# Attention and MLP on one core: where the tiles begin in a partition

## The chip, the cores and the metric

The kernel runs on one core of one Trainium2 chip. The metric is the device time of one execution in microseconds (us); lower is better.

## What is computed

Eight batches, eight heads, 576 positions, head size 64. Attention is causal by blocks of 64 positions, and its output goes through a layer norm and a two-layer MLP with a residual:

```python
scores = q @ k.T / sqrt(64);  scores = where(block_i >= block_j, scores, -1e9)
attn = exp(scores - max);     attn = attn / (sum(attn) + 1e-9)
x = (attn @ v).transpose(0, 2, 1, 3).reshape(8, 576, 512)
xn = (x - mean(x)) / sqrt(var(x) + 1e-6) * g_ln
out = x + relu(xn @ w_ch1) @ w_ch2          # 512 -> 2048 -> 512
```

All is float32.

## The kernel before

The work is cut into tasks; a planner written in Python (`Plan.run`) simulates the five engines and writes out one fixed order for each. There are two large parts.

**Attention**, 32 pairs of heads. For each pair TensorE makes the scores (`s`, line 388) in plain float32, VectorE adds the mask and takes the maximum (line 403), ScalarE takes the exponential (line 406), TensorE transposes the result (`tr`, line 415) and multiplies it with `v` (`o`, lines 421 and 425). The first block of each head goes a way of its own (lines 527 to 552). In the same time the MLP's weights are loaded and decoded, each into a high and a low part (`w1h`, `w1l`, `w2h`, `w2l`).

**MLP**, 9 groups of 512 rows, 16 steps `j` in each. Its operands have the type `fp32r`. The normalised rows lie in a high and a low part of a tile `xq` (groups 0, 2, 4, 6, 8) or `xp` (groups 1, 3, 5, 7). A step has 12 matmuls into `hp` (lines 675 to 677), a ReLU on ScalarE that writes the high part of `hhl` (line 683), a subtraction on VectorE that writes its low part (line 685), and 12 matmuls into `y` (lines 692 to 694), which TensorE runs after the `hp` of a later step:

```python
nc.tensor.matmul(hp.t, w1h[:, c, jf], xh.t[:, c], start=(c == 0), stop=False)
...
nc.tensor.matmul(ys[s].t, hh.t[:, sl], w2h, start=(j == 0), stop=False)
```

The second operand is the stationary one, 128 columns, which is loaded ahead of its matmul (the rows call this load `PEld`); the third is the moving one, which streams through. In each of these matmuls the moving operand is 512 columns of 4 bytes that lie in a row: 2048 bytes in each partition, and its start is the start of its tile plus a multiple of 2048. So `hp` streams `xq` or `xp`, and `y` streams `w2h` or `w2l`.

SBUF is handed out from the pools in the order in which they are opened, within a pool in the order in which tags are first used, each tile right behind the one ahead of it. The constants end at byte 1152 of a partition; `sums_all` (1024 bytes), `ident` (512), `never` (4352) and `g_sb` (2048) follow, so that the first weight tile begins at 9088 = 4 x 2048 + 896, and all tiles of a multiple of 2048 bytes behind it keep that 896, until a tile of another size comes. The tiles begin here (bytes past a multiple of 2048, and in brackets past a multiple of 256):

| tiles | before | changed |
|---|---|---|
| weights, `pt0`, `st_w2h`, `st_w2l` | 896 (128) | 0 (0) |
| `pu`, `hhl`, `v0` | 896 (128) | 0 (0) |
| `pab`, `xp`, `pt1`, `xre`, `ot`, `xrf`, `xn`, `xt` and their like | 1088 (64) | 0 (0) |
| `xnt`, `xq` | 1344 (64) | 0 (0) |
| `raw`, `qk0`, `wr` (two buffers) | 896, 1408 (128) | 0, 512 (0) |
| `v` (two buffers) | 1920, 384 (128) | 1024, 1536 (0) |
| `ident`, `never`, `g_sb` | 128, 640, 896 (128) | the same |

Of the kernel before, what the change touches and what calls it, by code (L numbers as in the profile page):

```python
# [9 lines left out]
F32 = mybir.dt.float32  # L10
F32R = mybir.dt.float32r
I32 = mybir.dt.int32
# [6 lines left out]
P = 128  # L19
# [35 lines left out]
class Plan:  # L55
# [5 lines left out]
    def add(self, eng, cost=None, fn=None, r=(), w=(), prio=0.0, size=0, alloc=(), mode=128):  # L61
        k = Task(eng if isinstance(eng, dict) else {eng: (cost, fn)}, prio, size)
        k.mode = mode
        before = {}
        for x in r:
            before.update(dict.fromkeys(x.writers))
        for x in w:
            before.update(dict.fromkeys(x.readers))
        for x in r:
            x.readers.append(k)  # L70
        for x in w:
            x.writers.append(k)
        for x in before:
            x.next.append(k)
        k.left = len(before)
        k.uses = list(dict.fromkeys(x.root for x in (*r, *w, *alloc)))
        for x in k.uses:
            x.users += 1
        k.allocs = [x for x in dict.fromkeys(x.root for x in (*w, *alloc)) if x.make]
        self.tasks.append(k)  # L80
        return k
# [101 lines left out]
def attn_mlp_kernel(ctx: ExitStack, tc: tile.TileContext, qk, qk0, v, v0, w1, w2, g, out):  # L183
# [9 lines left out]
    NPAIR, _, _, S = qk.shape  # L193
# [8 lines left out]
    const = ctx.enter_context(tc.tile_pool(name="const", bufs=1))  # L202
    sb = ctx.enter_context(tc.tile_pool(name="sb", bufs=1))
    dram = ctx.enter_context(tc.tile_pool(name="dram", bufs=2, space=bass.MemoryType.DRAM))
    psum = ctx.enter_context(tc.tile_pool(name="psum", bufs=1, space=PSUM))
    plan = Plan()
    add = plan.add

# [14 lines left out]
    def kind(name, shape, dtype, bufs, space=None, tag=None):  # L223

        tag = tag or name
        plan.free.setdefault(tag, bufs)

        def make():
            return (space or sb).tile(shape, dtype, name=name, tag=tag, bufs=bufs)

        def new():
            x = Buf((tag,), make)
            if tag not in ("tr", "x"):
                x.after, last[tag] = last.get(tag), x
            return x
        return new
# [3 lines left out]
    steps = {}  # L240
    new_tr, new_s1, new_hp, new_o = (kind(n, [P, 512], F32, 4, psum, "tr") for n in ("tr", "s1", "hp", "o"))

    new_raw, new_qk0 = kind("raw", [P, 2, S], F32, 2), kind("qk0", [P, 8, 2, 64], F32, 2, None, "raw")
    new_v = kind("v", [P, 5, P], F32, 2)
    new_pab, new_xp = kind("pab", [P, 2048], F32, 2), kind("xp", [P, NC, TW], F32R, 2, None, "pab")
    new_pu, new_hhl = kind("pu", [P, 1024], F32, 2), kind("hhl", [P, 2, 512], F32R, 2, None, "pu")
    new_pt0 = [kind("pt0", [P, 2, 4, 2, P], F32, 1, const, t) for t in ("w1h3", "w1l3")]
# [6 lines left out]
    new_xw = kind("xw", [512, P], F32, 8, dram)  # L254
    new_v0 = kind("v0", [P, 512], F32, 1)
    new_xq = kind("xq", [P, NC, TW], F32R, 2)
    new_nm = kind("nm", [P, 8], F32, 6)
    sums_all = const.tile([P, B, 4, 4, 2], F32, name="sums_all")
    new_st = kind("st", [P, 8], F32, 2)
    new_norm = kind("norm", [P, 16], F32, 3)  # L260
    xd = [kind("xd", [4 * P, 512], F32, B, dram)() for _ in range(B)]
    xd0 = [kind("xd0", [P, DM], F32, B // 2, dram)() for _ in range(B // 2)]

# [6 lines left out]
    gb = Buf()  # L270
    gsrc = bass.AP(tensor=g.tensor, offset=g.offset, ap=[[0, P], [1, DM]])
    add("SP", .45, lambda: nc.sync.dma_start(out=g_sb, in_=gsrc), w=[gb], prio=150, size=P * 2048)
    if WARM:
        warm = new_tr()

        def rouse():
            for _ in range(WARM):
                nc.tensor.transpose(warm.t[:, 0:P], ident, ident)
        add("PE", .2 * WARM + .5, rouse, w=[warm], prio=0)
# [12 lines left out]

    stages = ["w2h3", "w2l3"]
    new_stage = {n: kind("st_" + n, [P, 2048], I32, 1, const, n) for n in stages}
    new_word = kind("wr", [P, 1024], I32, 2, None, "raw")
    staged, staged_last = [0], []

    def decode(j, second, prio, k=0, parts=1):
# [413 lines left out]
def _run_one(arrays):  # L712
    import numpy as np
    import concourse.bacc as bacc
    from concourse.bass_utils import run_bass_kernel_spmd

    nc = bacc.Bacc("TRN2", target_bir_lowering=False, num_devices=1, dynamic_dma_scratch_size=1024)
    args = {n: nc.dram_tensor(n, a.shape, mybir.dt.from_np(a.dtype), kind="ExternalInput").ap()
            for n, a in arrays.items()}
    for n in ("w1", "w2"):  # L720
        args[n] = args[n].bitcast(I32)
    args["out"] = nc.dram_tensor("out_t", (36, P, 512), F32, kind="ExternalOutput").ap()
    with tile.TileContext(nc) as tc:
        attn_mlp_kernel(tc, *args.values())
    r = run_bass_kernel_spmd(nc, [arrays], core_ids=[0])
    return np.asarray(r.results[0]["out_t"])
# [35 lines left out]
```

## Time and profile before

| | us |
|---|---|
| median of 3 runs | 1117.52 (1116.17 to 1118.71) |
| the profiled execution | 1117.89 |
| its span, first to last instruction | 1116.1 |
| outside the span (difference) | 1.8 |

TensorE is busy in 99% of the span, VectorE in 47%, ScalarE in 32%, GpSimd in 12%; the mean share of the DMA engines is 33%. [...]

### The profile page before, as it was taken

To read this page: it belongs to the slowest core of one execution; us is meant where nothing else is said; L and a number is where in the kernel's file an instruction comes from. 1 tells how busy PE (TensorE), PEld (TensorE's weight loads), DVE (VectorE), ACT (ScalarE), POOL (GpSimd) and SP (SyncE) were. 2 spreads that over 40 slices of the span, in tenths; PEclk is the share of its full clock that TensorE was granted. 3 is DMA by queue.
4 is the path that set the end of the run, shared out by engine and by line. 5 is a ranking of instruction groups with operands and counts; after the bars stand their busy time and mean duration, and the time that the engine had idled before them with its cause. 6 is when DMAs were issued, how large, how long until landed. Compare 5 with 4: busy or idle time off the path is not lost.

```text
span 1116.1 us, 16345 instructions
## 1 busy us (share of the span) xinstructions
PE 1102.7 (99%) x6288; PEld 874.0 (78%) x6288; DVE 526.8 (47%) x1244; ACT 356.4 (32%) x880; POOL 130.0 (12%) x192
## 2 busy tenths in 40 slices
PE   9999999999999999999999999999999999999998
PEld 6767777777777888888888888888888888888886
DVE  6899988888866144135126126116215314412111
ACT  7989898997632111111111101111111111111110
POOL 1223423330035001001001001000000100100000
PEclk9999999999999999999999999999999999999999
DMA  6687765664263043034015006005105203301000
GB/s 206 208 200 238 225 221 184 207 194 147 83 149 98 1 87 64 1 72 80 1 49 102 1 13 127 13 0 118 34 1 104 48 1 83 69 1 39 1 1 38
DMA packets 205086, 97.80 MB, mean 88 GB/s; under 512 B 155728, under 2 KB 184400, under 8 KB 205008
## 3 DMA queue, kind: packets, MB, share of 16 engines
q1 hardware_dynamic: 205008, 96.76, 32.6%
q8 instruction: 49, 0.80, 0.3%
q14 instruction: 29, 0.24, 0.1%
HBM read 68.42 MB, written 28.31 MB: 87 GB/s over the span
## 4 chain that ended last, share of the span: by engine, by line
PE 82%; DVE 7%; ACT 6%; issue 2%; DMA 1%; POOL 1%; SPq 1%; DVEq 0%; POOLq 0%; ACTq 0%
PE hp L676 12%; PE hp L677 12%; PE hp L675 12%; PE y L693 11%; PE y L692 11%; PE y L694 11%; PE s L388 4%; PE tr L415 3%; PE o L425 3%; ACT pab L406 2%; ACT pt L217 2%; ACT pu L406 2%; PE o L421 1%; DVE pab L403 1%; DVE pu L403 1%
## 5 line engine op out<-in xcount | busy, mean ns | idle before, releaser
L685 DVE SCALAR_TENSOR_TENSOR hhl<-hp,hhl 128x512 fp32r<-128x512 f32 x144 | 99.6, 691 | 488.4 <-ACT hhl L683 488.3
L683 ACT ACTIVATE hhl<-hp 128x512 fp32r<-128x512 f32 x144 | 86.1, 598 | 695.2 <-PE hp L677 690.9
L694 PE MATMUL y<-w2h,hhl 128*128 128x512 f32 x576 | 224.3, 389 | 2.1 <-DVE hhl L685 2.1
L693 PE MATMUL y<-w2l,hhl 128*128 128x512 f32 x576 | 225.7, 392 | 0.0
L692 PE MATMUL y<-w2h,hhl 128*128 128x512 f32 x576 | 224.7, 390 | 0.0
L694 PEld LDWEIGHTS y<-w2h,hhl 128*128 128x128 f32 x576 | 108.2, 188 | 25.9 <-DVE hhl L685 2.8
L692 PEld LDWEIGHTS y<-w2h,hhl 128*128 128x128 f32 x576 | 108.0, 188 | 25.3
L693 PEld LDWEIGHTS y<-w2l,hhl 128*128 128x128 f32 x576 | 108.0, 188 | 23.7
L675 PE MATMUL hp<-xq,w1h 128*128 128x512 f32 x320 | 126.5, 395 | 0.0
L676 PE MATMUL hp<-xq,w1h 128*128 128x512 f32 x320 | 126.1, 394 | 0.0
L677 PE MATMUL hp<-xq,w1l 128*128 128x512 f32 x320 | 126.1, 394 | 0.0
L675 PE MATMUL hp<-xp,w1h 128*128 128x512 f32 x256 | 100.9, 394 | 0.0
L676 PE MATMUL hp<-xp,w1h 128*128 128x512 f32 x256 | 100.9, 394 | 0.0
L677 PE MATMUL hp<-xp,w1l 128*128 128x512 f32 x256 | 100.9, 394 | 0.0
L388 PE MATMUL s<-raw 64*128 64x320 f32 (+4 forms) x640 | 95.4, 439 | 0.7 <-DVE nm L403 0.6
L406 ACT ACTIVATE pab<-pab,nm 128x576 f32<-128x576 f32 (+1 forms) x128 | 91.5, 729 | 4.1 <-DVE nm L403 4.0
L388 PEld LDWEIGHTS s<-raw 64*128 64x128 f32 x640 | 58.3, 189 | 38.6 <-issue 32.4
L403 DVE CUSTOM_DVE_ANT_0 pab<-s,never 128x576 f32<-128x576 f32 (+1 forms) x128 | 82.6, 684 | 2.1 <-PE s L388 2.1
L425 PE MATMUL o<-pt,v 128*64 128x256 f32 (+1 forms) x768 | 80.4, 344 | 0.0
L425 PEld LDWEIGHTS o<-pt,v 128*64 128x64 f32 x768 | 56.9, 137 | 26.0
L658 POOL TENSOR_TENSOR norm<-norm 128x4 f32<-128x4 f32 x27 | 10.7, 398 | 570.2 <-DVE norm L652 568.8
L217 ACT COPY pt<-tr 128x512 f32<-128x512 f32 x139 | 72.0, 587 | 2.6 <-PE tr L415 2.5
(95 smaller groups left out, 1275.3 us busy)
## 6 DMA issues: line engine op xcount, KB each, us to landing
raw<-qk SPq DMA_DIRECT2D x32, 576.0 KB, 5.0
v<-v SPq DMA_DIRECT2D x32, 320.0 KB, 3.2
xw<-xnt SPq DMA_DIRECT2D x144, 64.0 KB, 2.0
xt<-xw SPq DMA_DIRECT2D x36, 256.0 KB, 2.8
xd<-ot SPq DMA_DIRECT2D x32, 256.0 KB, 3.9
st_w2h<-w SPq DMA_DIRECT2D x14, 512.0 KB, 5.3
st_w2l<-w SPq DMA_DIRECT2D x14, 512.0 KB, 4.7
xrf<-xd SPq DMA_DIRECT2D x80, 64.0 KB, 2.5
```

The costliest lines, as they stand in the source:

```text
L217: e.copy(out=out, in_=in_)
L388: nc.tensor.matmul(x, raw.t[HALF[h], 0, col], raw.t[HALF[h], 1, at:at + x.shape[1]], start=True, stop=True)
L403: add("DVE", dve(n) + .01, lambda: nc.vector.tensor_tensor_reduce(out=p.t[:, part(i, h)], in0=s.t[:, cols], in1=hide, scale=-0.125, scalar ...
L406: add("ACT", act(n, True) + .14, lambda: nc.scalar.activation(out=p.t[:, part(i, h)], in_=p.t[:, part(i, h)], func=AF.Exp, bias=nm.t[:, at ...
L425: nc.tensor.matmul(o.t[HALF[h], at + lo:at + 256], v_sb.t[:, ck, HALF[h]], rhs(h), start=False, stop=(n == len(steps) - 1), skip_group_che ...
L675: nc.tensor.matmul(hp.t, w1h[:, c, jf], xh.t[:, c], start=(c == 0), stop=False)
L676: nc.tensor.matmul(hp.t, w1h[:, c, jf], xl.t[:, c], start=False, stop=False)
L677: nc.tensor.matmul(hp.t, w1l[:, c, jf], xh.t[:, c], start=False, stop=(c == NC - 1))
L685: add("DVE", dve(TW), lambda hp=hp, hh=hh, hl=hl: nc.vector.scalar_tensor_tensor(out=hl.t, in0=hp.t, scalar=0.0, in1=hh.t, op0=ALU.max, op ...
L692: nc.tensor.matmul(ys[s].t, hh.t[:, sl], w2h, start=(j == 0), stop=False)
L693: nc.tensor.matmul(ys[s].t, hh.t[:, sl], w2l, start=False, stop=False)
L694: nc.tensor.matmul(ys[s].t, hl.t[:, sl], w2h, start=False, stop=(j == NJ - 1))
```

## The change

No instruction is added, removed or moved: with line numbers left aside, the two programs have the same instructions in the same order on every engine, with the same waits. What differs is the addresses in SBUF. A pool `odd` is opened last, and the tiles whose size is no multiple of 2048 bytes go there (`raw`, `qk0`, `wr`, `nm`, `st`, `norm`), or, for `v`, into the first pool, where two buffers of 2560 bytes and 128 bytes of padding (`even`) bring the weights to 14336 = 7 x 2048. All else behind that keeps a multiple of 2048; the table above has the starts. PSUM is as before.

```diff
     psum = ctx.enter_context(tc.tile_pool(name="psum", bufs=1, space=PSUM))
+    odd = ctx.enter_context(tc.tile_pool(name="odd", bufs=1))
...
-    new_raw, new_qk0 = kind("raw", [P, 2, S], F32, 2), kind("qk0", [P, 8, 2, 64], F32, 2, None, "raw")
-    new_v = kind("v", [P, 5, P], F32, 2)
+    new_raw, new_qk0 = kind("raw", [P, 2, S], F32, 2, odd), kind("qk0", [P, 8, 2, 64], F32, 2, odd, "raw")
+    new_v = kind("v", [P, 5, P], F32, 2, const)
...
-    new_nm = kind("nm", [P, 8], F32, 6)
+    new_nm = kind("nm", [P, 8], F32, 6, odd)
     sums_all = const.tile([P, B, 4, 4, 2], F32, name="sums_all")
-    new_st = kind("st", [P, 8], F32, 2)
-    new_norm = kind("norm", [P, 16], F32, 3)
+    new_st = kind("st", [P, 8], F32, 2, odd)
+    new_norm = kind("norm", [P, 16], F32, 3, odd)
...
+    const.tile([P, 32], F32, name="even")
...
-    new_word = kind("wr", [P, 1024], I32, 2, None, "raw")
+    new_word = kind("wr", [P, 1024], I32, 2, odd, "raw")
```

## Rows read from the trace of the kernel before

**Rows 1.** Stages: length, busy time (instructions) by engine, granted clock, DMA share, GB/s

```profile
0.00:300.00 300.00, 293.32 (x2727) 218.10 (x2728) 256.31 (x775) 254.26 (x698) 79.81 (x73) 1.00 0.64 197
300.00:339.02 39.02, 36.91 (x218) 29.04 (x216) 28.63 (x55) 13.97 (x30) 14.30 (x20) 1.00 0.54 122
339.02:1110.12 771.10, 771.09 (x3341) 626.11 (x3342) 239.13 (x412) 88.16 (x153) 35.88 (x100) 1.00 0.20 43
1110.12:1116.10 5.98, 1.35 (x6) 0.77 (x5) 2.73 (x4) 0.00 (x0) 0.00 (x0) 1.00 0.46 175
```

**Rows 2.** The chain that ended last, from 339.1 to 1110.1 us: shares by line

```profile
by line: PE hp L676 16.8%; PE hp L677 16.8%; PE hp L675 16.8%; PE y L693 16.6%; PE y L692 16.5%; PE y L694 16.5%
```

**Rows 3.** Matmuls of hp (first row), then of y, in the last stage

```profile
339.02:1112.00 772.98, 410.26 (x1668) 1.00 0.20 43
...
339.02:1112.00 772.98, 404.52 (x1678) 1.00 0.20 43
```

**Rows 4.** TensorE in order of time, a step with xq: start, duration, line

```profile
499.31 0.39 PE L675 MATMUL hp<-xq,w1h 128*128 128x512 f32 x1
...
502.11 0.39 PE L692 MATMUL y<-w2h,hhl 128*128 128x512 f32 x1
```

**Rows 5.** The same, a step with xp, and ScalarE's ReLU of that step

```profile
587.92 0.39 PE L675 MATMUL hp<-xp,w1h 128*128 128x512 f32 x1
...
590.49 0.39 PE L677 MATMUL hp<-xp,w1l 128*128 128x512 f32 x1
590.73 0.39 PE L692 MATMUL y<-w2h,hhl 128*128 128x512 f32 x1
590.95 0.40 PE L693 MATMUL y<-w2l,hhl 128*128 128x512 f32 x1
...
592.11 0.39 PE L692 MATMUL y<-w2h,hhl 128*128 128x512 f32 x1
...
593.24 0.39 PE L694 MATMUL y<-w2h,hhl 128*128 128x512 f32 x1
593.47 0.39 PE L675 MATMUL hp<-xp,w1h 128*128 128x512 f32 x1
...
590.92 0.60 ACT L683 ACTIVATE hhl<-hp 128x512 fp32r<-128x512 f32 x1 [4.94 <-PE hp L677]
```

**Rows 6.** The chain in a head pair: start, length, instructions

```profile
31.41 2.77 PE tr L415 x24
...
34.87 1.51 PE o L425 x16
...
36.82 0.65 PE o L425 x8
```

**Rows 7.** Weight loads: busy us, mean ns of one, idle before

```profile
L675 PEld LDWEIGHTS hp<-xp,w1h 128*128 128x128 f32 x256 | 47.9, 187 | 11.4
...
L415 PEld LDWEIGHTS tr<-ident,pab 128*128 128x128 f32 x512 | 55.3, 141 | 3.9 <-ACT pt L217 1.3 <-issue 0.2
```

**Rows 8.** VectorE's writes of hhl and xq: ns min/median/max

```profile
L685 DVE SCALAR_TENSOR_TENSOR hhl<-hp,hhl x144: 651/692/693, 316.3 to 1106.7; 128x512 fp32r<-128x512 f32 x144
...
L643 DVE TENSOR_TENSOR xq<-xt,xq x20: 650/691/693, 85.9 to 969.3; 128x512 fp32r<-128x512 f32 x20
```

**Rows 9.** The chain ahead of the last stage

```profile
334.97 1.40 DVE w1h L219
...
336.97 1.32 issue
338.29 0.69 DVE hhl L685
...
339.03 0.50 PE y L694
```

**Rows 10.** TensorE's waits from 339.1 to 1110.1 us, all of them

```profile
PE y L694 <- DVE hhl L685: 2.1, 1, 2.1
```

## The prediction

> **What bounds the kernel now.** I read the stages first, then the chain that ended last, then single matmuls. The stages [rows 1] show attention to about 300 us, a mixed stretch to 339.02, an MLP stage of 771.10 us, and a tail of 5.98. In the MLP stage TensorE is busy throughout, VectorE for 239.13 us of it and ScalarE for 88.16; the granted clock is 1.00, which is 2.4 GHz. The chain in that stage [rows 2] is nothing but the six matmul lines, three of `hp` and three of `y`, and the only wait of TensorE on another engine listed there is the one that ends as the stage begins [rows 10]. So 69% of the span is the number of these matmuls times the distance between their starts. The reader should look at that distance, since the change moves no instruction and can act only through addresses.
>
> Twelve `hp` matmuls take 502.11 - 499.31 = 2.80 us when they stream `xq` and 590.73 - 587.92 = 2.81 us with `xp` [rows 4, 5]: 233.3 ns each, at 2.4 GHz 560 clocks for 512 columns. The last six `y` of the step take 593.47 - 592.11 = 1.36 us [rows 5], 226.7 ns each, 544 clocks. What differs between the two kinds? Not the load of weights for the next matmul: from the last `hp` to the first `y`, while `hhl` is loaded, it is 590.73 - 590.49 = 0.24 us, and from the last `y` to the next `hp`, while `w1h` is loaded, 593.47 - 593.24 = 0.23; the rounding allows 233 and 227, so the distance goes with what the matmul itself streams. Both kinds stream 2048 contiguous bytes of the same type. But `xq` and `xp` begin 64 bytes past a multiple of 256, and `w2h` and `w2l` 128 past. I count clocks above 512: 48 for the offset 64, 32 for the offset 128.
>
> One reading fits both with no free constant: the stream is fetched to the end of the 256-byte block in which its last byte lies, at one 4-byte column a clock. From 64 it runs over 2048 + 192 bytes, 560 columns; from 128 over 2048 + 128, 544. It is inferred from two offsets only, so I keep others below.
>
> Plain float32 in attention is a check. There a column takes two clocks, and a fetch with a little surplus would stay hidden. L425 has 16 instructions on `pt0` (offset 128) in 1.51 us and 8 on `pt1` (offset 64) in 0.65 [rows 6]. They run as two heads side by side: 8 streams, six of 256 and two of 128 columns, and 4 streams, two of each. At two clocks a column that is 1493 and 640 ns; 17 and 10 ns are left, 2 to 3 ns for a stream at either offset. So float32 matmuls show no cost of the offset, and a floor of about 2.5 ns that nothing here removes.
>
> **The change part by part.** All parts are addresses, and they come in three kinds.
>
> *What the MLP streams.* `xq`, `xp` and the four `w2` parts all go to offset 0. By the reading above nothing is left above 512 columns: 213.3 ns, plus the 2.5 ns floor seen in attention, 215.8. The stage has 1668 `hp` and 1678 `y` [rows 3]. The saving is 1668 x (233.33 - 215.83) = 29.2 us and 1678 x (226.67 - 215.83) = 18.2 us, in all 47.4. Bounds: without the floor 213.3 ns, 33.4 + 22.4 = 55.7 us; if a sixteen-column unit stays over (560 and 544 are both multiples of 16), 528 columns or 220.0 ns, 22.2 + 11.2 = 33.4 us. I take 215.8, since the floor is in rows.
>
> [...]
>
> *What TensorE loads, and what other engines touch.* A weight load of `hp` is recorded with 187 ns [rows 7], under 215.8, and the record is no floor on the distance: 24 transposes with loads of 141 ns each run in 2.77 us, 115 ns each [rows 6, 7]. VectorE takes 692 ns to write `hhl` (offset 128) and 691 to write `xq` (offset 64) [rows 8], so its time does not hang on the offset: nothing. The first `y` of a step are a little slow: from 590.73 to 592.11 six take 1.38 us, not 1.36, while ScalarE writes `hhl` from 590.92 to 591.52 [rows 5]. That is 0.02 us in each of 139 steps, some 2.8 us in all, which could go or stay; I leave it.
>
> *Attention and its loads.* `raw`, `v`, `pab` and the staging tiles begin at multiples of 256 now. TensorE is idle for 300 - 293.32 = 6.7 us of that stage [rows 1], so no faster transfer or evacuation can give more than that. No row prices a loss. The matmuls there show no cost of the offset, so I take 0.
>
> What hides the rest: of the 9 x 16 x 24 = 3456 MLP matmuls 3346 come after 339.02 and 110 before, and there the chain runs through VectorE's cast of 1.40 us, 1.32 us of issue, and the subtraction at 338.29 [rows 9]. Shorter matmuls ahead of it only wait longer, so I count nothing for them. After it VectorE is needed for 239 of what would be 724 us; no wait follows from that load.
>
> Sum, against the profiled execution: 1117.89 - 47.4 = 1070.5 us. That execution is 0.4 us above the median of the runs, so about 1070 for a median.
>
> **The rivals.**
>
> *Only the odd 64 bytes cost.* Fixed 32 clocks for every `fp32r` matmul, from whatever source (the load of the next weights, say, which ends 187 ns after it starts, leaving some 40 ns to the next `y`), and 16 more when a stream begins off a multiple of 128 bytes. This fits as well, with two constants. For it: `y` is already at a multiple of 128. Against it: float32 shows no such fixed part with loads of the same size. Then `hp` falls to 226.7 and `y` stays: 1668 x 6.67 = 11.1 us, 1106.8 us.
>
> *One unit is left over.* The 220.0 ns worked out above: 1084.5 us.
>
> *Addresses don't matter, the change does nothing.* `hp` and `y` also go to different PSUM tiles, and that could make the 6.7 ns. For it: the tiles of both kinds are contiguous, and every engine row I compared takes the same at both offsets. Against it: clocks above 512 that fit the offsets to the clock. 1117.9 us.
> [...]
>
> *Slower: the surplus grows towards offset 0.* Two points, 48 clocks at 64 and 32 at 128, lie on a line that gives 64 at 0, as if a stream that begins on a block still fetched one block more. Then all matmuls take 576 clocks, 240.0 ns: 1668 x 6.67 + 1678 x 13.33 = 33.5 us more, 1151.4 us. It decides for slower as soon as the surplus at 0 is above 40 clocks, the mean of now. Against it: no byte of that block is needed. For it: no tile begins at 0 now, so no row shows that case.
>
> **How the numbers follow.** Chances: 215.8 ns at both kinds 0.56 (its own range 1058 to 1076: the floor gone, the slow `y` gone, or some transfer in attention better or worse); one unit left 0.07; `hp` alone 0.18; nothing 0.11; slower 0.08. A measurement of this kernel can tell about 0.2% from no change, 2.2 us. Faster is 0.56 + 0.07 + 0.18 = 0.81, the same 0.11, slower 0.08. The range for 8 in 10 holds the first three, from 1058 to 1109.
>
> **What would show it.** In the changed trace twelve `hp` from the first L675 row to the first L692 row of a step (two lines further down in the changed file): 2.59 us if right, 2.72 for `hp` alone, 2.80 for nothing, 2.88 for slower; the twelve `y` after it 2.59 to 2.61 against 2.74 now. Attention must end where it ended, near 300 us, and the first unbroken `hp` stream begin near 339. The chain of the MLP stage must still be six matmul lines; if VectorE's subtraction or a transfer shows in it, the shorter distance has uncovered a wait. The prediction is wrong if `y` does not move: then the offset of 128 cost nothing, and the 32 clocks have another source.

## The result, and the profile after

| | before | changed |
|---|---|---|
| median of 4 runs each, us | 1118.12 (1116.17 to 1118.90) | 1103.95 (1103.25 to 1105.42) |
| the profiled execution, us | 1117.89 | 1104.63 |
| its span, us | 1116.1 | 1102.8 |

The ratio of the times is 0.9878, with a 95% interval of 0.9860 to 0.9896: about 1.2% faster. The forecast was 1070, so the direction was right and the gain 14 us where 48 were expected.

The stages of the changed kernel, to set beside [rows 1] (length, busy us and instructions of PE, PEld, DVE, ACT and POOL, granted clock, DMA share, GB/s):

```profile
0.00:300.00 300.00, 292.96 (x2722) 217.03 (x2723) 256.17 (x775) 253.56 (x696) 79.39 (x73) 1.00 0.63 196
300.00:339.57 39.57, 37.23 (x222) 29.56 (x220) 29.16 (x55) 14.50 (x32) 14.35 (x20) 1.00 0.53 123
339.57:1096.90 757.33, 757.33 (x3341) 627.32 (x3342) 239.49 (x412) 88.16 (x153) 35.28 (x100) 1.00 0.20 44
1096.90:1102.80 5.90, 1.39 (x7) 0.81 (x5) 2.73 (x4) 0.00 (x0) 0.00 (x0) 0.97 0.46 178
```

The whole difference lies in the third row. With 3341 matmuls in both traces the MLP stage takes 757.33 us in place of 771.10, 13.8 less. It begins 0.55 us later (339.57, before 339.02), and the tail is 0.08 shorter: -13.8 + 0.55 - 0.08 = -13.3, which is 1102.8 - 1116.1.

Matmuls recorded with 0.39 us start about 0.23 us apart, so their records overlap; what one takes is counted here from its start to the next one's. TensorE of the changed kernel in order of time, two `y` groups with an `hp` group (on `xp`) between them. All files that are two lines longer than the one before have `hp` at L677 to L679 and `y` at L694 to L696:

```profile
581.33 0.39 PE L694 MATMUL y<-w2h,hhl 128*128 128x512 f32 x1
...
582.69 0.39 PE L694 MATMUL y<-w2h,hhl 128*128 128x512 f32 x1
...
584.05 0.39 PE L677 MATMUL hp<-xp,w1h 128*128 128x512 f32 x1
...
586.77 0.39 PE L694 MATMUL y<-w2h,hhl 128*128 128x512 f32 x1
```

Twelve `hp` take 586.77 - 584.05 = 2.72 us, where [rows 5] had 2.81: 226.7 ns each, 544 clocks. (A clock is 1/2.4 = 0.417 ns here, as in the prediction, at a granted clock of 1.00. Float32 streams take two of these for a further column: the two L425 pieces of [rows 6] differ by four streams of 256 columns, (1.51 - 0.65) us / 4 = 215 ns, and `full` in experiment 1 has 20.60 us / 48 = 429 ns for 512, so 0.84 ns a column.) Twelve `y` take 584.05 - 581.33 = 2.72 us, where they took 2.74. Of these the first six take 1.36 us (before 1.38) and the last six 1.36, as before. So `hp` fell to what `y` had, `y` stayed, and its slow beginning is gone.

The chain of that stage, by line, then TensorE's waits in it (us in total, times, longest), and the chain ahead of it (start, length, what):

```profile
by line: PE y L696 16.7%; PE y L695 16.7%; PE hp L678 16.7%; PE hp L679 16.7%; PE hp L677 16.7%; PE y L694 16.7%
```

```profile
PE y L696 <- DVE hhl L687: 2.3, 1, 2.3
```

```profile
335.51 1.40 DVE w1h L220
...
337.52 1.31 issue
338.84 0.69 DVE hhl L687
...
339.57 0.50 PE y L696
```

These answer to [rows 2, 10, 9]. Still six matmul lines, now with equal shares, and no wait that was not there before.

By terms: 1668 `hp` x 6.67 ns = 11.1 us. The `y` of the stage come in 131 unbroken runs (a few runs hold two steps), and the first six of each run took 0.02 us more before: 2.6 us. Together 13.7, against 13.8 in the stage.

### The profile page after: what moved, and what is told of

Read it like the earlier page. It is cut to its first block, busy times and chain, and to the rows that moved or that the text cites. A ratio compares the mean times of both kernels' runs of the same rounds, so it can differ in the third digit from the quotient of the medians.

```text
span 1102.8 us, 16345 instructions
## 1 busy us (share of the span) xinstructions
PE 1088.9 (99%) x6288; PEld 874.7 (79%) x6288; DVE 527.6 (48%) x1244; ACT 356.2 (32%) x880; POOL 129.0 (12%) x192
## 4 chain that ended last, share of the span: by engine, by line
PE 81%; DVE 8%; ACT 5%; DMA 2%; issue 2%; POOL 1%; SPq 0%; DVEq 0%; ACTq 0%; POOLq 0%
PE y L696 11%; PE hp L678 11%; PE hp L679 11%; PE hp L677 11%; PE y L695 11%; PE y L694 11%; PE s L390 3%; PE o L427 3%; PE tr L417 3%; ACT pab L408 2%; ACT pt L218 2%; ACT pu L408 2%; PE o L423 2%; DVE pab L405 1%; DVE pu L405 1%
## 5 line engine op out<-in xcount | busy, mean ns | idle before, releaser
L696 PE MATMUL y<-w2h,hhl 128*128 128x512 f32 x576 | 224.3, 389 | 2.3 <-DVE hhl L687 2.3
L694 PE MATMUL y<-w2h,hhl 128*128 128x512 f32 x576 | 224.1, 389 | 0.0
L696 PEld LDWEIGHTS y<-w2h,hhl 128*128 128x128 f32 x576 | 108.2, 188 | 25.5 <-DVE hhl L687 3.1
L694 PEld LDWEIGHTS y<-w2h,hhl 128*128 128x128 f32 x576 | 108.2, 188 | 22.5
L677 PE MATMUL hp<-xq,w1h 128*128 128x512 f32 x320 | 124.9, 390 | 0.0
L678 PE MATMUL hp<-xq,w1h 128*128 128x512 f32 x320 | 124.5, 389 | 0.0
L679 PE MATMUL hp<-xq,w1l 128*128 128x512 f32 x320 | 124.5, 389 | 0.0
L677 PE MATMUL hp<-xp,w1h 128*128 128x512 f32 x256 | 99.6, 389 | 0.0
L678 PE MATMUL hp<-xp,w1h 128*128 128x512 f32 x256 | 99.6, 389 | 0.0
L679 PE MATMUL hp<-xp,w1l 128*128 128x512 f32 x256 | 99.6, 389 | 0.0
```

The lines of the kernel that those rows point to most:

```text
L678: nc.tensor.matmul(hp.t, w1h[:, c, jf], xl.t[:, c], start=False, stop=False)
L679: nc.tensor.matmul(hp.t, w1l[:, c, jf], xh.t[:, c], start=False, stop=(c == NC - 1))
L696: nc.tensor.matmul(ys[s].t, hl.t[:, sl], w2h, start=False, stop=(j == NJ - 1))
```

## Experiments

The result leaves 544 clocks for both kinds at offset 0, so "fetched to the end of the 256-byte block" is gone: it asked for 512. Two theories were set against each other; both give 560 clocks for the old `hp` and 544 for all other settled fp32r matmuls of the two traces.

- *Edge*: only the moving operand's own start counts. A stream that begins off a multiple of 128 bytes costs 16 clocks; 32 are paid always.
- *Relation*: while a matmul streams, TensorE loads the stationary operand of the next one: in the trace of the kernel before, the load for the `y` that starts at 590.73 us [rows 5] is recorded from 590.49 on, the start of the `hp` ahead of it (the line below), and loads are busy for 626.11 us of the 771.10 in which the matmuls follow each other without a break [rows 1]. What counts is the distance from the stationary operand's start to the moving one's, modulo 256 bytes. In the kernel before it is 64 - 128, that is 192, for `hp` (`xq` or `xp` against `w1`) and 128 - 128 = 0 for `y` (`w2` against `hhl`).

```profile
590.49 0.19 PEld L692 LDWEIGHTS y<-w2h,hhl 128*128 128x128 f32 x1
```

**1. Matmuls by themselves, at many starts.** A small kernel: 24 equal matmuls, back to back, for each of 37 settings.

```python
COUNT = 24
...
x, s = a[:, o // 4:o // 4 + n], b[:, p // 4:p // 4 + m]
for _ in range(COUNT):
    nc.tensor.matmul(ps[0:m, 0:n], s, x, start=True, stop=True)
```

> This kernel computes nothing of the reference: it runs 24 equal matmuls in a row for each of 37 settings (start of the moving operand, start of the stationary one, columns, type) and writes a dummy output. Edge theory (a stream that begins off a multiple of 128 bytes costs 16 clocks more, and an fp32r matmul of 512 columns has 32 clocks of another source): 226.7 ns between starts with the moving operand at 0, 128, 256 and 1024 bytes, 233.3 at 64, 192 and 320, whatever the start of the stationary one. Relation theory (what counts is where the stream begins relative to the load that runs beside it): 226.7 only where both begin alike, so moving 64 with stationary 64 gives 226.7, and stationary 64 with moving 0 gives 233.3. If the 32 clocks come from the load of the next weights, 64 or 32 stationary columns bring 512 columns to about 216 ns; if they come from the stream, the number of columns sets them, and 480 columns show another surplus. Plain float32 at 0 and at 64 bytes: the same, as in attention.

Its chain (start, length, setting, instructions), with 24 matmuls in each row but the float32 ones, which are recorded as two instructions each:

```profile
14.14 5.44 PE mova L53 x24
...
30.74 5.49 PE movd L53 x24
...
41.84 5.60 PE movf L53 x24
...
53.06 5.60 PE movh L53 x24
58.66 5.46 PE movi L53 x24
...
86.17 5.60 PE stad L53 x24
...
108.30 5.48 PE botha L53 x24
113.78 5.48 PE bothb L53 x24
119.26 5.60 PE bothc L53 x24
...
133.09 2.93 PE lenb L53 x24
136.01 4.17 PE lenc L53 x24
140.18 4.96 PE lend L53 x24
145.13 5.20 PE lene L53 x24
150.33 5.37 PE lenf L53 x24
155.70 2.83 PE odda L53 x24
...
173.21 5.51 PE wida L53 x24
...
184.28 5.20 PE half L53 x24
189.48 20.60 PE full L53 x48
210.08 20.61 PE fullodd L53 x48
```

| row | moving / stationary start, bytes | clocks a matmul |
|---|---|---|
| `mova` | 0 / 0 | 5.44 us / 24 = 226.7 ns, 544 |
| `movd`, `movf`, `movh` | 64, 128, 192 / 0 | 549, 560, 560 |
| `movi` | 256 / 0 | 546; 544 after the first few |
| `stad` | 0 / 64 | 560 |
| `botha`, `bothb` | 64 / 64, 128 / 128 | 548 |
| `bothc` | 64 / 128, as `hp` before | 560 |
| `half` | bfloat16, 0 / 0 | 520 |
| `full`, `fullodd` | float32, 0 / 0 and 64 / 0 | 2 instructions, 1030 each |

`stad` streams from 0 and pays 560; `botha` streams from 64 and pays 548. Both are against *edge*, which looks at the stream alone, and `movf` is too. Starts that are equal modulo 256 take 544 at 0 and 548 at 64 and 128, and at these two 544 in the whole kernels of experiment 3; experiment 7 shows where this ends. After a change of setting the first matmuls can be slow: `movi`, which follows a row at distance 192, takes 0.02 us more in all than `mova` (5.46 and 5.44). In the trace its first five take 226, 235, 229, 232 and 231 ns, the rest 227. Float32, in two instructions of 1030 clocks for each matmul, shows no difference (20.60 and 20.61 us).

**2. All starts moved, the distance kept.** In the kernel before, 64 bytes ahead of the first weight tile move every wide tile: `w1`, `w2` and `hhl` from 128 to 192 past a multiple of 256, `xq` and `xp` from 64 to 128.

```diff
     g_sb = const.tile([P, DM], F32, name="g_sb")
+    const.tile([P, 16], F32, name="lead")
```

> The kernel before, with 64 bytes of padding ahead of the weights, so that w2 and hhl begin at 192 past a multiple of 256 and xq and xp at 128. Edge theory: hp falls to 226.7 ns and y rises to 233.3, about 1118 us, no change. Relation theory: the distance between streams and weights is that of before, so hp stays at 233.3 and y at 226.7; no change either, but the other way round in the trace. If only a multiple of 2048 helps: hp and y both at least as slow as before.

TensorE in order of time (one line longer than before: `hp` from L676, `y` from L693):

```profile
587.84 0.39 PE L676 MATMUL hp<-xp,w1h 128*128 128x512 f32 x1
...
590.64 0.39 PE L693 MATMUL y<-w2h,hhl 128*128 128x512 f32 x1
...
593.38 0.39 PE L676 MATMUL hp<-xp,w1h 128*128 128x512 f32 x1
```

Still 2.80 us for `hp` and 2.74 for `y`; 1118.17 us (10 runs) against 1117.67, ratio 1.0006 [0.9997, 1.0015]. The streams of `hp` begin at a multiple of 128 now and those of `y` no longer do; neither time moved. *Edge* would have exchanged them.

**3. All wide tiles alike at 128, and alike at 64.** The changed kernel with a longer piece of padding ahead of the weights.

```diff
-    const.tile([P, 32], F32, name="even")
+    const.tile([P, 64], F32, name="even")
```

and, for 64:

```diff
-    const.tile([P, 32], F32, name="even")
+    const.tile([P, 48], F32, name="even")
```

> The changed kernel with 128 bytes more of padding: every wide tile begins 128 bytes past a multiple of 2048. Edge theory: hp and y both at 226.7 ns, 1104 us, as the changed kernel. If the multiple of 2048 (or of 256) is what counts: slower than the changed kernel, up to the 1118 us of before. If the slow first y of a step came from ScalarE writing a tile at 128, they are back, and the time is about 1107 us.

> The changed kernel with 64 bytes more of padding: every wide tile begins 64 bytes past a multiple of 2048. Edge theory (a stream off a multiple of 128 bytes costs 16 clocks): hp and y both at 233.3 ns, about 1125 us. Relation theory (what counts is that the stream and the load beside it begin alike, modulo 256 bytes): both at 226.7 ns, 1104 us, as the changed kernel.

At 128: 1103.35 us against 1117.67, ratio 0.9874 [0.9858, 0.9891]. At 64: 1103.55 us against 1117.31, ratio 0.9868 [0.9852, 0.9885]. TensorE in order of time, at 64:

```profile
580.18 0.39 PE L694 MATMUL y<-w2h,hhl 128*128 128x512 f32 x1
...
582.90 0.39 PE L677 MATMUL hp<-xp,w1h 128*128 128x512 f32 x1
...
585.62 0.39 PE L694 MATMUL y<-w2h,hhl 128*128 128x512 f32 x1
```

Twelve `hp` and twelve `y` take 2.72 us each, at 128 as well. So starts at 2048 bytes, or at 256, are not what helps: at 64, where *edge* has every fp32r matmul at 560 clocks, the whole gain is there.

**4. 64 bytes in the kernel before, and nothing else.** One 64-byte tile, ahead of the first `pab` (whose place `xp` shares, and behind which `xq` lies), brings `xp` and `xq` from 64 to 128 past a multiple of 256, where `w1`, `w2` and `hhl` are. `raw`, `v`, the weights and all else ahead of that place stay where they were, and none of the MLP's operands is at a multiple of 256.

```diff
-    last = {}
+    last, lead = {}, []
...
+            if tag == "pab" and not lead:
+                lead.append(sb.tile([P, 16], F32, name="lead"))
             return (space or sb).tile(shape, dtype, name=name, tag=tag, bufs=bufs)
```

> The kernel before with one 64-byte tile of padding ahead of pab: xq and xp go from 64 to 128 past a multiple of 256, where w1, w2 and hhl already are; nothing begins at a multiple of 2048. Relation theory: all matmuls at 226.7 ns and no slow first y, so the whole gain, about 1104 us. Edge theory gives the same for hp, but keeps the slow y if they came from ScalarE writing hhl at 128: about 1107 us. If a multiple of 2048 is needed: 1118 us.

TensorE in order of time, and ScalarE's ReLU of the same step:

```profile
587.73 0.39 PE L677 MATMUL hp<-xp,w1h 128*128 128x512 f32 x1
...
590.45 0.39 PE L694 MATMUL y<-w2h,hhl 128*128 128x512 f32 x1
...
591.81 0.39 PE L694 MATMUL y<-w2h,hhl 128*128 128x512 f32 x1
...
593.17 0.39 PE L677 MATMUL hp<-xp,w1h 128*128 128x512 f32 x1
```

```profile
590.65 0.60 ACT L685 ACTIVATE hhl<-hp 128x512 fp32r<-128x512 f32 x1 [4.84 <-PE hp L679]
```

`hp` 2.72 us, `y` 2.72 us; 1103.27 us, ratio 0.9870 [0.9854, 0.9886], the same as the whole change. The first six `y` take 591.81 - 590.45 = 1.36 us, though the ReLU writes `hhl`, at the offset of before, from 590.65 to 591.25, across them.

**5. The change with the old distance put back.** The changed kernel with 192 bytes at that place: `xq` and `xp` at 192, all weights and `hhl` at 0, as in the change.

```diff
-    last = {}
+    last, lead = {}, []
...
+            if tag == "pab" and not lead:
+                lead.append(sb.tile([P, 48], F32, name="lead"))
             return (space or sb).tile(shape, dtype, name=name, tag=tag, bufs=bufs)
```

> The changed kernel with 192 bytes of padding ahead of pab: weights and hhl at 0, xq and xp 192 bytes past a multiple of 256, the same distance as before the change (64 less 128). Relation theory: hp at 233.3 ns, slow first y back, about 1118 us. Edge theory: 192 is off a multiple of 128, so hp at 233.3, but y even at 226.7: about 1115 us.

TensorE in order of time (two lines longer than the changed kernel: `hp` from L679, `y` from L696):

```profile
590.01 0.39 PE L679 MATMUL hp<-xp,w1h 128*128 128x512 f32 x1
...
592.81 0.39 PE L696 MATMUL y<-w2h,hhl 128*128 128x512 f32 x1
...
594.19 0.39 PE L696 MATMUL y<-w2h,hhl 128*128 128x512 f32 x1
...
595.55 0.39 PE L679 MATMUL hp<-xp,w1h 128*128 128x512 f32 x1
```

`hp` 2.80 us, the first six `y` 1.38, the last six 1.36: the pattern of [rows 5] is back. 1117.66 us, ratio 1.0003 [0.9993, 1.0012]: all of the gain undone by the place of `xq` and `xp` alone.

**6. Another distance.** The kernel before with `nm` in tiles of 64 bytes in place of 32, which moves `xq` and `xp` to 0 past a multiple of 256 (1536 and 1280 past a multiple of 2048) with the weights still at 128.

```diff
-            return (space or sb).tile(shape, dtype, name=name, tag=tag, bufs=bufs)
+            return (space or sb).tile([P, 16] if name == "nm" else shape, dtype, name=name, tag=tag, bufs=bufs)[tuple(slice(0, x) for x in shape)]
```

> The kernel before with one edit: each nm tile takes 64 bytes and not 32, which moves xq and xp (and all behind nm) to multiples of 256, while w2 and hhl stay at 128. Edge theory: hp and y both at 226.7 ns. The slow first y of a step tell two causes apart: if they hang on hhl and w2 at 128 they stay (2.8 us) and the time is about 1107 us; if they hang on the tiles at 64 they go, 1104 us. Relation theory: hp and its weights don't begin alike, so hp stays near 233 ns, and the time near 1118 us.

TensorE in order of time:

```profile
588.98 0.39 PE L692 MATMUL y<-w2h,hhl 128*128 128x512 f32 x1
...
591.71 0.40 PE L675 MATMUL hp<-xp,w1h 128*128 128x512 f32 x1
...
594.50 0.39 PE L692 MATMUL y<-w2h,hhl 128*128 128x512 f32 x1
```

1114.88 us, ratio 0.9977 [0.9968, 0.9987]. A multiple of 256 for the streams of `hp` did not bring them to 226.7 ns: twelve take 2.79 us. In the trace they take 234 and 223 ns, then 238 and 229 in turns, and at distance 128 `movf` has 233.3 on average (5.60 us / 24), 560 clocks. *Relation* had named no gain. By the starts in the two traces `hp` gives 1.1 us and the first `y` of a run 0.7; the other 1.2 of the 3.0 by which the span is shorter (1113.1 against 1116.1 us) lie ahead of the MLP stage, which begins at 337.84 us and not 339.02. Why it does is not known.

**7. Finer starts, and where the 32 clocks left come from.** Two more small kernels of the same form, 32 matmuls for each of 30 settings and 36 for each of 23.

> This kernel computes nothing of the reference: 32 equal matmuls in a row for each of 28 settings, and a dummy output. Relation theory: fp32r distances go with the distance of the two starts modulo 256 bytes, 544 clocks at 0 and near it, up to 560 elsewhere; with a stationary operand whose columns lie apart (steps of 2 to 16 elements) the load touches other places and the distance changes; when every other matmul loads from 64 or 128 bytes on, the distances alternate or lie between; bf16 and plain float32 show 518 and 1030 clocks at any distance, since they take half as many bytes a clock. Edge theory: 560 wherever the stream begins off a multiple of 128 bytes, and no effect of the stationary operand. If the 32 clocks that are left come from the load meeting the stream, some setting of the stationary operand brings fewer than 544.

> This kernel computes nothing of the reference: 36 matmuls in a row for each of 23 settings, and a dummy output; in some settings fp32r matmuls alternate with bf16 or float32 ones. What is asked is where the 32 clocks above 512 come from that are left with both starts alike. If they come from the load of the next fp32r weights that runs beside the stream: an fp32r matmul that is followed by a bf16 one, whose load is of another kind, takes about 518 clocks, at an offset of 128 bytes too, and only one that is followed by another fp32r matmul takes 544 (560 at 128). If they belong to the fp32r stream itself: 544 before a bf16 matmul as well. Fine starts of the stationary operand (4 to 28 bytes): values between 544 and 568 clocks; none below 544 if the alike start is the best there is.

Chain of the first of the two:

```profile
17.88 7.25 PE finea L54 x32
25.13 7.57 PE fineb L54 x32
...
70.01 7.33 PE againa L54 x32
...
136.24 7.82 PE stepd L54 x32
...
151.59 7.26 PE alta L54 x32
158.84 7.47 PE altb L54 x32
...
188.34 6.92 PE half L54 x32
195.26 6.91 PE halfoff L54 x32
```

Clocks are length / 32, at 2.4 to a ns. A moving start 4 bytes off (`fineb`) costs 568 against 544 (`finea`). Distance 64 gives 550 here (`againa`, 64 / 0), near the 549 of `movd`. The layout of the stationary operand counts too: with stationary columns 8 elements apart (`stepd`) it is 587, and when every second stationary operand lies 256 bytes further (`alta`) 544, 128 further (`altb`) 560. Bfloat16 has 519 at distance 0 and 518 at 192 (`half` and `halfoff`, 6.92 and 6.91 us). The same two starts can have two prices: 128 / 64, distance 64 too, took 5.59 us / 24, 559 clocks, in the first small kernel, and 550 in this one; 0 / 16 took 5.45 us / 24, 545 clocks, in the first and 8.40 us / 36, 560, in the last one.

Equal starts are not enough either. The last small kernel has five more settings with both operands at the same place, `samea` at 4 bytes and `samee` at 192:

```profile
173.83 8.55 PE samea L49 x36
...
207.38 8.17 PE samee L49 x36
```

At 192 it is 545 clocks, at 4 it is 570, and between them 8, 16 and 48 take 555, 552 and 559. So the price of 544 at equal starts is shown for 0, 64, 128 and 192, and for this shape alone. With 64 stationary columns equal starts cost 552 (64 / 64, 7.36 us / 32) and unequal ones 548 (64 / 0, 7.31); with 256 moving columns it is 293 at 0 / 0 (`lenb`, 2.93 us / 24) and 283 at 64 / 0 (`odda`, 2.83), the first matmuls of each row counted in.

No fp32r setting of 512 columns went below 544. Halving the stationary columns gave 551 (`wida`, 5.51 us / 24), so fewer of them do not bring the 32 clocks down. They are not a constant: 256, 384 and 512 moving columns took 293, 417 and 544 in the first small kernel (`lenb`, `lenc`, `mova`), 37, 33 and 32 too many with the first matmuls of each row counted in, but 448, 480 and 496 took 496, 520 and 537 (`lend`, `lene`, `lenf`), which is 48, 40 and 41 too many. The last small kernel let other types take turns with fp32r: bfloat16 (`mixed` at distance 0, `mixedoff` at 128, `plain` bfloat16 alone) and float32 (`wide` at 0, `wideoff` at 128):

```profile
26.77 8.28 PE mixed L49 x36
35.05 8.30 PE mixedoff L49 x36
43.34 7.77 PE plain L49 x36
...
67.78 19.56 PE wide L49 x54
87.34 19.62 PE wideoff L49 x54
```

In turns with bfloat16 the distance shows no price: 8.30 against 8.28 us, where 18 matmuls at 560 clocks for 544 would add 0.12. But the pair takes 230 ns a matmul, where halves of 226.7 and 215.8 make 221.2, so taking turns has a price of its own, and the 32 clocks could not be told from it. Float32 alone took 20.60 us / 24 = 858.3 ns a matmul. With 18 of these taken off, an fp32r matmul in `wide` has 228 ns left and in `wideoff` 232, estimates from these rows: beside float32 loads about 32 clocks stay, and some of the price of the distance. Where the 32 come from is inconclusive.

## Why the prediction was wrong

- **What bounds the kernel: right.** The stage is 3341 matmuls times their distance, before and after, and nothing else entered its chain.
- **The step that failed** is "the distance goes with what the matmul itself streams", with the load of the next weights ruled out. It rested on the two seams between `hp` and `y`, 0.24 and 0.23 us [rows 5], read to 0.01 us where the difference looked for is 0.007. And the load began at 128 in both kinds, `w1` or `hhl`. So the rows held one operand still and moved the other; they could not tell the stream's own offset from its offset against the load. The prediction's own sign of being wrong came: the settled `y` did not move. Experiments 2 and 5 tell the two apart: the same distance at other offsets costs the same, and moving `xq` and `xp` alone undoes everything.
- **The 256-byte block and its 215.8 ns** fell with it; no run shows a fetch to the end of a block. Two points fitted to the clock, 48 at 64 and 32 at 128, were not two values of one function: the 48 are the 32 that the settled `y` had and both kinds have after the change (226.7 ns), and 16 for the distance of 192. By terms: `hp` saved 6.67 ns a matmul, not 17.5, 11.1 us for 29.2; a settled `y` saved nothing, for 18.2.
- **The slow first `y`** were set beside ScalarE's write of `hhl` and left out of the sum, as 0.02 us in 139 steps, 2.8 us; in 131 runs it is 2.6. Experiment 4 has that write in the same place and no slow `y`; experiment 5 has them back. In the trace of the kernel before, the first five of a run take 226, 236, 228, 233 and 231 ns in the median, the rest 227. `movi` has nearly the same row (226, 235, 229, 232, 231, then 227) after the same change of distance, from 192 to 0, with no other engine at work. So they go with the change of distance from `hp` to `y`, and they are about a fifth of the gain.
- **The rival "only the odd 64 bytes cost"** gave 1106.8, the nearest time, by a mechanism that experiments 2 and 3 refute: with it the kernel at 64 would have gained nothing. The measured time lies in the range from 1058 to 1109 us only because the range held this rival, which is luck and not a mechanism that was right.
- **The 215.8 ns themselves** were the author's estimate, 512 columns at one a clock (213.3 ns) and the 2.5 ns left over in the float32 rows. Bfloat16 took as long in an unbroken row of experiment 7 (7.77 us / 36 = 215.8 ns); no run shows it for fp32r, which took 226.7 at best.
- **Right besides:** attention gained nothing (TensorE busy for 292.96 of its 300 us, 293.32 before, and experiment 4 reached the same time with `raw` and `v` where they were); the 110 matmuls ahead of the stage gave nothing that shows, since that stretch became 0.55 us longer, not shorter; no new wait came up.

Open remain where the 32 clocks above 512 come from, why the same two starts can have one price here and another there, why equal starts cost more at 4 to 48 bytes, and the 1.2 us ahead of the stage in experiment 6. Whether it is the operand loaded beside the stream or the matmul's own stationary operand that counts was not settled: in the whole kernels both begin at the same place modulo 256. No version beats the changed kernel; 64 bytes in the kernel before equal it.

## What to carry to other kernels

For fp32r matmuls of 512 moving and 128 stationary columns, let the moving operand and the stationary operands that go with it start at the same multiple of 64 modulo 256 bytes: that was worth 6.7 ns a matmul here, 226.7 for 233.3 at distance 192. A few bytes of padding ahead of one tile may do it, and where that common place lies didn't matter at 0, 64 and 128 (2.72 us for twelve each) and 192 (8.17 us / 36 = 226.9 ns, by itself). For other shapes, and for starts between these, measure first: equal starts were not the best there. Look for it in the trace as matmuls of one shape with two distances between starts. Before a cost is put down to one operand, find rows in which the other one varies, and if there are none, a small kernel that varies both costs less than a theory fitted to two points.

## What the runs showed of the hardware

Fp32r matmuls of 512 moving and 128 stationary columns took 233.3 ns where the moving operand starts at distance 192 from the stationary one and 226.7 at distance 0, in whole kernels (2.80 and 2.72 us for twelve) and by themselves (`movh` 5.60 us / 24, `mova` 5.44). With stationary columns 8 elements apart it was 244 ns (`stepd`, 7.82 us / 32, 587 clocks). At a distance of 256 bytes the mean was 546 clocks (`movi`), at 128 it was 560 (`movf`). Bfloat16 (`half` and `halfoff`, 519 and 518 clocks) and float32 (`full` and `fullodd`, distance 0 and 64, 20.60 and 20.61 us for 24) showed no cost of the distance. That the load beside the stream is what makes the difference in fp32r was not shown.
